# q, k and O turned by crossbar DMA transposes instead of TensorE, in an order made by a list scheduler

## The chip, the cores and the metric

The kernel runs on one core of one Trainium2 chip. The metric is device time in microseconds (us), the median of several executions. Here only fast runs are compared with fast runs; a run counts as slow when it is over 1.5% above the fastest of the same kernel. Engine names are those of the profile: PE is TensorE, PEld its weight loads, DVE is VectorE, ACT is ScalarE, POOL is GpSimd, SP is SyncE (here only an issuer of DMAs; SPq is its queue).

## The reference, cut to what matters

Sliding-window causal attention over 8 batches, 8 heads, 576 positions and 64 dimensions, with a window of 64 keys; the heads are then laid side by side as 4608 tokens of 512 features, which go through two dense layers with a SiLU between them. All inputs and the output are float32; both kernels compute in bf16.

```python
scores = scale * np.matmul(q, k.transpose(0, 1, 3, 2))
mask = (rel >= 0) & (rel < 64)                      # rel = query position - key position
attn = softmax(np.where(mask, scores, -1e9))
x = np.matmul(attn, v).transpose(0, 2, 1, 3).reshape(4608, 512)
h = x @ w_in                                        # 512 -> 2048, "first layer"
out = (h * sigmoid(h)) @ w_out                      # 2048 -> 512, "second layer"
```

## The kernel before

A *unit* is one pair of heads of one batch (32 units); a *group* is 192 query positions of a unit (96 groups); a *token tile* is 512 tokens (9 tiles, numbered from 0). The matmuls of both kernels are written for q and k with the 64 dimensions on the partitions, and those of the first layer for the attention output O with its features on the partitions, so all three are turned. Before, TensorE turns them: six matmuls against an identity for each q and k of a unit, three for the O of a group, each followed by an eviction from PSUM.

```python
def transposes(u, nm, copies):
    pst = at_ps.tile([128, 6, 96], BF16, name="pst", tag="ap")
    for m in range(6):
        nc.tensor.matmul(pst[:, m, :], lhsT=t[:, m, :], rhs=ident[0:96, 0:96], is_transpose=True, ...)
    # ... q: two evictions (VectorE, ScalarE) into qbd; k: one into kt

def scores(u, g):
    # ... three matmuls into sp
    nc.scalar.activation(out=e, in_=sp, func=ACTF.Exp, scale=scale)
    nc.vector.tensor_mul(e, e, mask0 if g == 0 else mask)

def values(u, g):
    # ... three matmuls into pv
    nc.vector.reciprocal(out=rc, in_=...)
    for hh in range(2):
        nc.vector.tensor_mul(ob[...], pv[...], rc[...].to_broadcast([64, 3, 64]))

def to_bridge(u, g):
    for x in range(3):
        nc.tensor.matmul(op[:, x, :], lhsT=ob[:, x, :], rhs=twoi, start=(x == 0), stop=(x == 2))
    nc.scalar.copy(out=bridge[pj][:, c0:c0 + 192], in_=op.rearrange("p x i -> p (x i)"))
```

The order is made by hand. The first layer of tile 0 is cut in two, so that it starts when the first 192 positions of batch 0 are there. After that, the q and k turns of the next units are placed among the first-layer matmuls of a tile, and 12 or 8 groups of attention among its second-layer matmuls:

```python
interleave(mm1(0, 0, 192), 7, first, lead=2)
# ...
for j in range(NTT):
    # ...
    interleave(mm1(j, 192, TT) if j == 0 else mm1(j), 6, ins, lead=30 if j == 0 else 4)
    interleave(mm2(j, j == 0), 3, attention_steps(part[j]), lead=2)
```

The softmax here doesn't subtract the row's maximum and nothing guards it: scores larger than these inputs give would overflow.

## Time and profile before

| | before |
|---|---|
| time, median of 3 | 396.05 us (395.33 to 396.76) |
| span of the profiled execution | 394.6 us |
| TensorE, VectorE, ScalarE, GpSimd busy | 329.4, 232.9, 206.3, 133.4 us |
| first matmul of the first layer | 41.5 us |
| first matmul of tile 1 | 89.2 us |

The last two rows are read from the timeline of TensorE. I use the second to cut every kernel into a **head** (start of the span to the first first-layer matmul of tile 1) and a **body** (from there to the end of the span): here 89.2 and 305.4 us.

These are lines of the page of the kernel before. The rows of digits are 40 equal slices, each digit the busy share of a slice in tenths; the rows with q0 and q1 are the DMA queues with packets, MB and share of the 16 DMA engines; the line after them is the chain that ended last, by engine; the last lines are groups of instructions (busy us and mean ns behind the bar, then the idle time before them). Of the names, e is the exponentials, pv the products with v, rc the reciprocals of their sums, obd (later ob) the normalised output, bridge the first layer's input, kraw a k that is turned but not yet in its place in kt.

```profile
PE 329.4 (83%) x2423; PEld 180.0 (46%) x2464; DVE 232.9 (59%) x596; ACT 206.3 (52%) x410; POOL 133.4 (34%) x185
...
PE   0046896999989997899779978998799889989995
...
DMA  9999999129901916382646456723710001001002
...
q0 software_dynamic: 45568, 11.28, 29.0%
q1 hardware_dynamic: 38336, 25.96, 24.4%
...
PE 51%; DVE 32%; ACT 6%; issue 5%; POOL 2%; DMA 2%; DVEq 0%; ACTq 0%; POOLq 0%
...
L169 DVE TENSOR_TENSOR e<-e,mask 128x384 bf16<-128x384 bf16 x96 | 43.0, 452 | 49.5 <-ACT e L168 47.1
L187 DVE TENSOR_TENSOR obd<-pv,rc 64x192 bf16<-64x192 f32 x192 | 68.2, 355 | 4.6
```

TensorE is close to full from the fifth slice on, and the DMA engines are full in the first seven slices (to about 69 us) and mostly half empty after that. The same in numbers, from the busy times by windows (after the window: us, busy us of the five engines with instruction counts, granted clock, DMA share, GB/s; the DMA share sums the time of packets and can be above 1):

```profile
0.00:41.50 41.50, 11.76 (x115) 9.32 (x116) 20.95 (x69) 15.39 (x28) 30.00 (x47) 0.99 1.24 205
...
89.20:268.00 178.80, 161.76 (x1185) 85.35 (x1208) 113.88 (x265) 101.81 (x193) 57.99 (x77) 1.00 0.55 109
```

In the head, the chain of the kernel before goes through a cast, six TensorE transposes and an eviction for each turn (start us, us, what):

```profile
8.91 7.15 DMA vv<-in_v_dram
...
19.75 0.42 DVE q_natb L126
20.22 0.68 PE pst L136 x6
20.92 0.75 DVE qbd L143
...
41.65 0.48 PE ps L226 x3
```

In a second-layer phase with 12 groups of attention, the chain that ended last runs through VectorE: reciprocal, two normalisations, mask, group after group. The columns are start us, us, and what.

```profile
149.54 0.21 DVE rc L184
149.77 0.04 DVE obd L187
149.81 0.33 issue
150.13 0.36 DVE obd L187
...
150.53 0.69 DVE ot L238
151.25 0.36 DVE e L169
```

Such a phase takes 25.9 us (141.9 to 167.8), of which TensorE is busy 21.0.

### The profile page before, as it was taken

The page shows a single profiled execution, that of the slowest core. Times are in us where ns is not written, and L with a number is a line of the kernel's source. Part 1 is how long each engine was busy: PE and PEld are TensorE (multiplying, and loading weights), DVE is VectorE, ACT ScalarE, POOL GpSimd, SP SyncE. Part 2 cuts the span into 40 slices and gives each one's busy share as a digit, 9 for nine tenths or more (in the row PEclk, how much of TensorE's full clock was granted, in tenths as well). Part 3 has the DMA queues.
Part 4 walks back from the last instruction along what each step waited for, and adds up shares of the span by engine and source line. Part 5 has one row for each costly group of instructions (what it writes and reads, how often), then busy time and mean ns, then how long its engine had stood idle before and what let it go on. Part 6 is the DMA issues. An engine that isn't in the chain of part 4 may idle for free.

```text
span 394.6 us, 6598 instructions
## 1 busy us (share of the span) xinstructions
PE 329.4 (83%) x2423; PEld 180.0 (46%) x2464; DVE 232.9 (59%) x596; ACT 206.3 (52%) x410; POOL 133.4 (34%) x185
## 2 busy tenths in 40 slices
PE   0046896999989997899779978998799889989995
PEld 0035773545454554354435543545355544454442
DVE  0467979967584649664984485539944790093011
ACT  2066775545842774367445752585357645742710
POOL 8756999123900029200950077004900000000000
PEclk9999899899999999999999999999999999999999
DMA  9999999129901916382646456723710001001002
GB/s 190 166 213 250 119 209 174 9 17 272 120 27 71 250 10 64 71 213 54 65 51 185 109 57 86 201 67 43 71 55 0 30 27 55 0 28 69 13 27 80
DMA packets 83935, 37.65 MB, mean 95 GB/s; under 512 B 40256, under 2 KB 78656, under 8 KB 83904
## 3 DMA queue, kind: packets, MB, share of 16 engines
q0 software_dynamic: 45568, 11.28, 29.0%
q1 hardware_dynamic: 38336, 25.96, 24.4%
q8 instruction: 19, 0.31, 0.3%
q14 instruction: 12, 0.10, 0.1%
HBM read 36.70 MB, written 9.44 MB: 117 GB/s over the span
## 4 chain that ended last, share of the span: by engine, by line
PE 51%; DVE 32%; ACT 6%; issue 5%; POOL 2%; DMA 2%; DVEq 0%; ACTq 0%; POOLq 0%
PE ps L226 28%; PE ps L250 15%; DVE obd L187 13%; DVE e L169 7%; DVE rc L184 4%; PE pst L136 4%; ACT L168 2%; DVE ot L238 2%; PE pv L177 2%; DMA vv<-in_v_dram 2%; ACT e L168 2%; DVE qbd L143 2%; ACT gt L233 1%; POOL vv L75 1%; DVE vv L151 1%
## 5 line engine op out<-in xcount | busy, mean ns | idle before, releaser
L250 PE MATMUL ps<-w_out_sb,gt 128*128 128x512 bf16 x551 | 141.5, 381 | 1.3 <-ACT gt L233 0.3
L226 PE MATMUL ps<-bridge,w_in_sb 128*128 128x512 bf16 (+2 forms) x624 | 135.2, 359 | 0.9
L233 ACT ACTIVATE gt<-ps 128x512 bf16<-128x512 f32 (+2 forms) x160 | 84.6, 555 | 46.8 <-PE ps L226 45.3
L75 POOL DMA_DIRECT2D vv<-in_v_dram x64 | 49.1, 773 | 131.4 <-PE pv L177 90.6
L226 PEld LDWEIGHTS <-w_in_sb 128*128 128x128 bf16 x640 | 58.8, 99 | 51.9 <-issue 0.8
L169 DVE TENSOR_TENSOR e<-e,mask 128x384 bf16<-128x384 bf16 x96 | 43.0, 452 | 49.5 <-ACT e L168 47.1
L187 DVE TENSOR_TENSOR obd<-pv,rc 64x192 bf16<-64x192 f32 x192 | 68.2, 355 | 4.6
L250 PEld LDWEIGHTS <-gt 128*128 128x128 bf16 x576 | 49.4, 98 | 41.1 <-issue 1.0
L168 ACT ACTIVATE e<-sp 128x384 bf16<-128x384 f32 x96 | 44.7, 491 | 33.9 <-PE sp L162 33.8
L238 DVE COPY ot<-ps 128x512 f32<-128x512 f32 x36 | 24.6, 690 | 55.9 <-PE ps L250 55.3
L202 ACT CAST bridge<-op 128x192 bf16<-128x192 f32 x96 | 30.6, 318 | 45.6 <-PE op L199 44.3
L177 PE MATMUL pv<-vv,e 128*128 128x130 bf16 x288 | 33.8, 228 | 11.9 <-DVE e L169 6.8
L144 ACT COPY qbd<-pst 64x576 bf16<-64x576 bf16 x32 | 20.3, 633 | 40.3 <-DVE qbd L143 40.3
L199 PE MATMUL op<-twoi,obd 128*128 128x64 bf16 x288 | 25.1, 197 | 17.9 <-DVE obd L187 15.5
L162 PEld LDWEIGHTS <-kt 128*128 128x128 bf16 x288 | 25.2, 104 | 24.0 <-issue 2.9
L136 PE MATMUL pst<-ident,q_natb 96*128 96x96 bf16 x192 | 14.4, 214 | 26.0 <-DVE q_natb L126 26.0
L162 PE MATMUL sp<-qbd,kt 128*128 128x128 bf16 x288 | 33.2, 231 | 3.1 <-ACT kt L147 1.4
L147 DVE COPY kt<-pst 128x576 bf16<-128x576 bf16 x28 | 21.1, 755 | 18.3 <-PE pst L136 18.3
L177 PEld LDWEIGHTS <-e 128*128 128x128 bf16 x288 | 21.9, 101 | 20.9 <-DVE e L169 10.8
L199 PEld LDWEIGHTS <-obd 128*128 128x128 bf16 x288 | 15.7, 99 | 33.2 <-DVE obd L187 32.8
L143 DVE COPY qbd<-pst 64x576 bf16<-64x576 bf16 x32 | 24.0, 749 | 11.1 <-PE pst L136 11.0
L126 POOL CAST q_natb<-q_nat 96x768 bf16<-96x768 f32 x28 | 24.7, 881 | 13.3 <-DMA q_nat<-in_q_dram 13.3
(37 smaller groups left out, 188.8 us busy)
## 6 DMA issues: line engine op xcount, KB each, us to landing
out_dram<-ot SPq DMA_DIRECT2D x36, 256.0 KB, 2.1
q_nat<-in_q_dram SPq DMA_DIRECT2D x28, 288.0 KB, 6.1
k_nat<-in_k_dram SPq DMA_DIRECT2D x28, 288.0 KB, 6.1
vv<-in_v_dram POOLq DMA_DIRECT2D x64, 64.0 KB, 3.3
w_in_sb<-in_moe_w_in_dram POOLq DMA_DIRECT2D x8, 256.0 KB, 7.5
w_out_sb<-in_moe_w_out_dram POOLq DMA_DIRECT2D x8, 256.0 KB, 7.1
q_nat<-in_q_dram POOLq DMA_DIRECT2D x4, 288.0 KB, 8.8
k_nat<-in_k_dram POOLq DMA_DIRECT2D x4, 288.0 KB, 9.0
```

The lines of the kernel that those rows point to most:

```text
L75: nc.gpsimd.dma_start(out=t[:, 1:9:2, hh * 65:hh * 65 + 64], in_=v[b, 2 * pj + hh, 0:512, :].rearrange("(c p) d -> p c d", p=128),)
L143: copies[0](out=d[0:64, 0], in_=src[0:64])
L162: nc.tensor.matmul(sp[:, x], lhsT=kt[i][:, t * 64:t * 64 + 128], rhs=qbd[i][:, :, t * 64:(t + 1) * 64], start=(x == 0), stop=(x == 2),)
L168: nc.scalar.activation(out=e, in_=sp, func=ACTF.Exp, scale=scale)
L169: nc.vector.tensor_mul(e, e, mask0 if g == 0 else mask)
L177: nc.tensor.matmul(pv[:, x, :], lhsT=e[:, x].rearrange("p h i -> p (h i)"), rhs=vv[i][:, 3 * g + x, :], start=(x == 0), stop=(x == 2),)
L187: nc.vector.tensor_mul(ob[p0:p0 + 64, :, p0:p0 + 64], pv[p0:p0 + 64, :, hh * 65:hh * 65 + 64], rc[p0:p0 + 64, :, hh:hh + 1].to_broadcast([ ...
L199: nc.tensor.matmul(op[:, x, :], lhsT=ob[:, x, :], rhs=twoi, start=(x == 0), stop=(x == 2))
L226: nc.tensor.matmul(ps[:, lo:hi], lhsT=w_in_sb[:, c, ft * 128:(ft + 1) * 128], rhs=bridge[c][:, t0 + lo:t0 + hi], start=(c == 0), stop=(c = ...
L233: nc.scalar.activation(out=gts[(j, ft)][:, lo:hi], in_=ps[:, lo:hi], func=ACTF.Silu)
L238: nc.vector.tensor_copy(out=ot, in_=ps)
L250: nc.tensor.matmul(ps[m], lhsT=gts[(j, f)][:, m * 128:(m + 1) * 128], rhs=w_out_sb[:, f, :], start=(f == 0), stop=(f == NFT - 1),)
```

## The change

The intent is to take 384 q and k transposes and 288 O turns off TensorE, and their evictions off VectorE and ScalarE, and to have the DMA do them from SBUF to SBUF with `dma_start_transpose` ("crossbar" transposes in what follows; 89 of them in the trace of the kernel after, whose result is correct): q straight into its place, k into a buffer from which VectorE copies it, O straight into the first layer's input. All of these transposes go through one queue, SP. The order of all work, on all engines and DMA queues, is no longer written by hand: a list scheduler runs before the kernel is built, with a duration for each operation, and issues in the order of its simulated clock.

The diff, cut to its core:

```diff
+class Plan:
+    def add(self, eng, cls, us, fn, deps=(), lat=0.08, gate=None, dma=None): ...
+    def run(self, rank):
+        # ... at each event, each free engine takes the ready operation with the lowest (rank, number)
+                    end = free[e] = now + op["us"]
+                    if op["dma"] is None:
+                        op["seen"] = end + op["lat"]
+                    else:
+                        pipe = max(pipe, end + 0.6) + op["dma"]      # one pipe for all DMAs
+                        op["seen"] = pipe + 1.2
...
-    def transposes(u, nm, copies): ...          # TensorE, PSUM, evictions
-    def to_bridge(u, g): ...                    # TensorE, PSUM, eviction
+    def turn_q(w, b, pj):                       # 48 rows, 24 blocks of 128 columns
+        nc.sync.dma_start_transpose(
+            out=qbd[b % NK][:, pj].rearrange("x h m p -> x (h m) p"),
+            in_=nbq[w][r:r + NPR].rearrange("p h m x -> p (h m x)"))
+    def turn_k(w, pj):                          # 48 rows, 12 blocks
+        nc.sync.dma_start_transpose(out=kraw[pj], in_=nbk[w][r:r + NPR].rearrange("p m x -> p (m x)"))
+    def place_k(eng, b, pj): ...                # VectorE copy kraw -> kt
+    def turn_o(o, b, g):                        # 64 rows, 12 blocks: 192 positions of all four head pairs
+                nc.sync.dma_start_transpose(
+                    out=bridge[:, a:z].rearrange("x n j i -> x (n j) i"),
+                    in_=obs[o % NOB][:, s:s + z - a].rearrange("p n j x -> p (n j x)"))
...
+                p.add("SP", "turn", 0.5, lambda pj=pj, w=w: turn_q(w, b, pj), cast_done[2 * pp] + busy, dma=1.0)
+                p.add("SP", "turn", 0.5, lambda pj=pj, w=w: turn_k(w, pj), ..., dma=0.5)
+            o_turn.append(p.add("SP", "turn", 0.5, lambda o=o, b=b, g=g: turn_o(o, b, g), ..., dma=0.8))
...
-    interleave(mm1(0, 0, 192), 7, first, lead=2)   # and the loop over tiles
+    p.run(dict(one=0, ld=3, turn=0, st=2, dma=1, cast=5, shift=4, place=3, s=1, pv=0, moe=3, exp=1, silu=0,
+               mask=1, norm=0, out=2))
```

Three smaller things come with it. The loads of q and k bring packets of 1 KB instead of 512 B, and v comes in one layout for all heads of a batch. The casts to bf16 run on ScalarE (on GpSimd before, after the first units). The first layer of tile 0 is no longer cut in two: it waits for all of batch 0.

## The prediction

> **What bounds the kernel now.** The page gives TensorE 83% busy, VectorE 59%, ScalarE 52%, DMA 53% by queue shares. The 1,152 MoE matmuls set the floor: where they run back to back (last tile, timeline 376.8 on: 16 in 3.45 us) one takes 0.216 us, 249 us in all. The other 146 us are three things.
>
> 1. Head: the first MoE matmul starts at about 41 us (timeline). VectorE waited 12.5 us for v loads merely to write ones columns (waits: vv L121), so its first q cast came at 19.7. The first token tile is then cut in two and mixed with attention; tile 1 starts only at 89.
> 2. Each later token tile takes 34 to 42 us (chain: 126.2, 168.0, 209.8, 247.7, 288.9) against 27.7 for the last one, which has nothing beside it. Six TensorE transposes cost 0.26 us of the stream (first-layer phase: groups of six matmuls every 1.55 instead of 1.30), 2 per head pair, up to 2.1 us a tile. The O turn costs about 0.1 us a group, scores plus values 0.36.
> 3. TensorE waits in second-layer phases for VectorE: 1.36 us a group (mask 0.452, reciprocal 0.194, two normals 0.355 each). One 12-group phase takes 26 us for 18 us of MoE and attention matmuls. The chain holds obd 13%, mask 7%, rc 4%.
>
> **Removed.** PE: 384 transposes (28.8 us busy) and 288 O turns (25.1 us). VectorE: q evictions 24.0 us, most clears; ScalarE: q evictions 20.3, bridge copies 30.6. PSUM buffers for both turns vanish.
>
> **Added.** 32 q, 32 k and about 25 O crossbar transposes on the SP queue, 18.9 MB. This trace has none. [...] each plus about 2 us to land (stores land in 2.1). No run here shows it yet. q/k packets double from 512 B to 1 KB[...]. ScalarE takes the casts (0.83 us each by the k cast seen here, about 50 us): its total stays near 205. VectorE falls from 233 to about 205.[...]
>
> **Critical path.** Clears precede v loads, so casts start near 6 us; turns, then 12 groups x 1.36 us on VectorE, then an O turn: first MoE matmul near 38 us, now with batch 0 complete. After it 249 us of MoE, 84 groups x 0.34 = 29 us of attention matmuls, 4 us tail: 320. Mismatch of the static order with real DMA latency, one exposed O turn before tile 1, and DMA contention: about 15 us more. **335 us, 8 in 10 between 313 and 372**; faster 0.87, same 0.06, slower 0.07. A 15% gain.
>
> **What would show it.** First MoE matmul at 34 to 44 us; tile 1 starting at 70 to 78, not 89; tiles of 30 to 34 us; TensorE gaps over 0.4 us largely gone beside attention; VectorE busy 195 to 215; O turns landing 2.5 to 4 us after issue; DMA share up to 60 to 80%.
>
> **What would make it wrong.** Transposes moving under about 100 GB/s: then q/k turns of a batch take over 20 us, the head grows by 10 to 20 us, and SP, in order, holds stores and loads behind them; the chain would show DMA qbd, kraw or bridge. Priorities tuned on wrong durations would show as PE waiting for ScalarE's casts ahead of silu (0.83 us each), or for bridge. If turns are faster and the model exact, 313.

The sum came to 320 us: 38 for the head, 249, 29 and 4; with about 15 more it is 335.

## The result and the profile after

| | before | after |
|---|---|---|
| time, median of 4 | 396.12 us (395.33 to 396.76) | 437.94 us (433.73 to 441.35) |
| span of the profiled execution | 394.6 us | 434.7 us |
| TensorE, VectorE, ScalarE, GpSimd busy | 329.4, 232.9, 206.3, 133.4 us | 308.0, 192.4, 192.0, 45.8 us |
| first matmul of the first layer | 41.5 us | 87.0 us |
| head (to tile 1) | 89.2 us | 127.5 us |
| body | 305.4 us | 307.2 us |

The change is slower: the ratio is 1.102, 95% interval 1.093 to 1.111. A ratio is the mean time of one kernel's fast runs over the mean of the other's fast runs of the same rounds, so it is not quite the ratio of the medians that I quote. (One of the four executions of after, the 441.35, counts as slow and is not in the ratio.) The result is correct in both.

So of the 40.1 us between the two spans, 38.3 are in the head and 1.8 in the body. Two things have to be explained: why the head grew, and why the body gained nothing although TensorE has less to do there.

The page of the kernel after, the lines that answer to those above:

```profile
PE 308.0 (71%) x1706; PEld 151.8 (35%) x1728; DVE 192.4 (44%) x484; ACT 192.0 (44%) x316; POOL 45.8 (11%) x55
...
PE   0000033099949999992999299969988868799996
...
DMA  9999999999896999799679997969742482401001
...
q1 hardware_dynamic: 100000, 46.02, 62.2%
q0 software_dynamic: 43776, 8.92, 26.7%
q10 hardware_dynamic: 1664, 1.57, 2.4%
...
L216 DVE COPY kt<-kraw 128x576 bf16<-128x576 bf16 x32 | 35.7, 1128 | 62.2 <-DMA kraw<-nbk 62.0
```

TensorE is idle or nearly so for eight slices, and later its row has single low digits (4, 2, 2), where before it has none below 7 from the eighth slice to the last but one. The DMA row is full or nearly so over two thirds of the span. The queue shares add up to 91%, where before they were 53%.

```profile
0.00:87.00 87.00, 9.78 (x73) 6.87 (x74) 26.55 (x72) 17.30 (x26) 25.89 (x35) 1.00 1.42 179
...
127.50:300.00 172.50, 147.72 (x828) 72.19 (x839) 92.51 (x232) 97.08 (x161) 15.96 (x16) 0.92 1.04 151
```

The clock of 1.00 in the first line says nothing: the first clock record of this trace is at 91 us.

The chain that ended last, in the head of the kernel after:

```profile
4.67 10.26 DMA nat<-in_q_dram
...
15.43 0.56 DVE nbq L201
16.01 1.79 SPq L205
17.84 6.46 SPq L205
...
34.24 6.15 SPq L205
40.44 8.48 SPq L205
...
49.65 1.40 SPq L212
51.10 9.28 DMA kraw<-nbk
60.41 1.13 DVE kt L216
61.58 0.82 PE sp L232 x6
...
77.10 9.74 DMA bridge<-ob
86.98 3.15 PE mp L277 x7
```

This is how to read it. The first q load lands at 15.0, its cast is done at 16.0. Then SP, which issues in program order, is held: L205 is the issue of one q transpose, and the four of batch 0 hold the queue for 1.8, 6.5, 6.2 and 8.5 us. They come in two pairs, each with its two k transposes (L212) behind it and with loads of batch 1 (L164) between. The last k transpose lands at 60.4, 9.3 us after its issue. Two groups of batch 0 have run by then (from 40.6); the ten that are left take 16.7 us, 1.67 us a group, and the last O transpose 9.7 us more. In the kernel before, the first q turn ran from 20.2 to 21.7 with its eviction, 1.5 us.

The waits of the kernel after (engine, line, what it waited for: us in all, times, longest) name the same two places:

```profile
PE sp L232 <- DVE kt L216: 66.9, 9, 40.6
DVE kt L216 <- DMA kraw<-nbk: 62.0, 15, 14.4
...
PE mp L277 <- DMA bridge<-ob: 26.8, 6, 11.6
```

In the body, five first layers wait for an O transpose (1.0 to 5.7 us each), and what follows a wait can start slowly. From the timeline of TensorE (start us, us, ..., count, then idle before and what ended it):

```profile
205.13 2.29 PE L277 MATMUL mp<-bridge,w_in_sb 128*128 128x512 bf16 x5 [5.65 <-DMA bridge<-ob]
```

Five matmuls took 2.29 us. At the full rate they take 1.08 (16 in 3.45 us on the last tile before). In this trace the granted clock is 0.50 from 200.25 to 210.49 us, so it came back 5.4 us after the matmuls began; it had fallen 0.8 us into the idle stretch, before which TensorE already had gaps of 0.95 and 2.15 us. The mean granted clock is 0.92 from 127.5 to 300 us, where the kernel before has 1.00. So this wait for DMA cost more than its own length: about 2.7 us more, an estimate (half of the 5.4 us at half clock). Over the body the clock stood at half for 38.6 us, in which TensorE was busy for 26.7; by the same estimate about 13 us are lost there.

### The profile page after: what moved, and what is told of

It reads as the page before. It is cut to its first block, busy times and chain, and to the rows that moved or that the text cites. A ratio compares the mean times of both kernels' runs of the same rounds, so it can differ in the third digit from the quotient of the medians.

```text
span 434.7 us, 4930 instructions
## 1 busy us (share of the span) xinstructions
PE 308.0 (71%) x1706; PEld 151.8 (35%) x1728; DVE 192.4 (44%) x484; ACT 192.0 (44%) x316; POOL 45.8 (11%) x55
## 3 DMA queue, kind: packets, MB, share of 16 engines
q0 software_dynamic: 43776, 8.92, 26.7%
## 4 chain that ended last, share of the span: by engine, by line
PE 56%; DMA 19%; DVE 11%; SPq 9%; issue 3%; ACT 2%; ACTq 0%; DVEq 0%
PE mp L277 30%; PE mp L286 19%; DMA bridge<-ob 9%; SPq L205 5%; DMA kraw<-nbk 5%; DVE ob L259 4%; DMA nat<-in_q_dram 3%; PE sp L232 3%; PE pv L249 3%; DVE kt L216 3%; SPq L212 2%; DVE ot L292 2%; DMA qbd<-nbq 1%; DVE rc L256 1%; SPq L164 1%
## 5 line engine op out<-in xcount | busy, mean ns | idle before, releaser
L277 PE MATMUL mp<-bridge,w_in_sb 128*128 128x512 bf16 x576 | 140.2, 404 | 34.8 <-DMA bridge<-ob 26.8
L283 ACT ACTIVATE g<-mp 128x512 bf16<-128x512 f32 x144 | 85.2, 597 | 134.6 <-PE mp L277 134.6
L286 PE MATMUL mp<-w_out_sb,g 128*128 128x512 bf16 x554 | 138.9, 381 | 1.2 <-issue 0.2
L286 PEld LDWEIGHTS <-g 128*128 128x128 bf16 x576 | 54.2, 98 | 50.8 <-issue 0.6
L259 DVE TENSOR_TENSOR ob<-pv,rc 64x192 bf16<-64x192 f32 x192 | 68.0, 354 | 4.6
L216 DVE COPY kt<-kraw 128x576 bf16<-128x576 bf16 x32 | 35.7, 1128 | 62.2 <-DMA kraw<-nbk 62.0
L292 DVE COPY ot<-mp 128x512 f32<-128x512 f32 x36 | 24.2, 689 | 85.1 <-PE mp L286 84.6
L201 ACT CAST nbq<-nat 112x768 bf16<-112x768 f32 x28 | 22.6, 827 | 18.6 <-DMA nat<-in_q_dram 14.6
L256 DVE RECIPROCAL rc<-pv 128x6 f32<-128x6 f32 x96 | 18.8, 195 | 26.5 <-PE pv L249 24.5
L199 ACT CAST nbk<-nat 112x768 bf16<-112x768 f32 x32 | 25.4, 830 | 11.2 <-DMA nat<-in_k_dram 10.4
L283 ACT ACT_TABLE_LOAD x8 | 10.3, 1283 | 0.1
```

The costliest lines, as they stand in the source:

```text
L199: eng(out=dst[:, h], in_=src[:, h])
L216: eng(out=kt[b % NK][:, 64 + pj * S:64 + (pj + 1) * S].rearrange("x (g p c) -> x g p c", g=NG, c=NC), in_=kraw[pj].rearrange("x (g c) p -> ...
L259: nc.vector.tensor_mul(obs[o % NOB][:, :, pj, 64 * hh:64 * hh + 64], pv[r, :, hh, 0:D], rc[r, :, hh:hh + 1].to_broadcast([64, 3, 64]),)
L277: nc.tensor.matmul(mps[mp], lhsT=w_in_sb[:, c, ft * 128:(ft + 1) * 128], rhs=bridge[:, n0:n0 + TB, c, :], start=(c == 0), stop=(c == NDC - 1),
L283: nc.scalar.activation(out=gts[gt], in_=mps[mp], func=ACTF.Silu)
L286: nc.tensor.matmul(mps[mp], lhsT=gts[gt][:, m * 128:(m + 1) * 128], rhs=w_out_sb[:, f, :], start=(f == 0), stop=(f == NFT - 1),)
```

## The experiments

Four theories, with what each would show:

- **The crossbar is slow in these shapes.** Alone on an idle DMA the transposes are already far slower than I had taken them to be. Then other shapes, or plain copies of the same bytes, give the time back.
- **The DMA is full.** The turns are late because loads lie ahead of them and beside them. Then taking loads away, or moving them, gives the time back.
- **The order is built on wrong durations.** The scheduler believes in 1.0 us for a q turn. Then true durations give a better order.
- **The O turn is the body's wait.** Then a first layer that does not wait for it gives the body's loss back.

The expectations are quoted; where they name a theory by a letter, C is the one of the wrong durations and F one that came up later, that the casts on ScalarE delay the rest. What each run was to tell apart is said in words beside it.

All results in one table. Ratios are against the kernel before in the same rounds; head and body are from the profiled execution of each, as defined above. Of the six of late, two were slow and are not in its ratio.

| run | what it is | us, median | ratio (95%) | head | body |
|---|---|---|---|---|---|
| before | | 396.12 | 1 | 89.2 | 305.4 |
| after | | 437.94 | 1.102 (1.093–1.111) | 127.5 | 307.2 |
| copy* | after, turns replaced by plain copies | 412.40 | 1.039 (1.033–1.044) | 125.8 | 283.5 |
| wide | after, turns of 128 rows | 409.54 | 1.033 (1.029–1.037) | 128.3 | 279.4 |
| no_w* | after, weights not loaded | 418.69 | 1.056 (1.051–1.062) | 111.1 | 305.9 |
| no_v* | after, v of batches 2 to 7 not loaded | 426.86 | 1.079 (1.073–1.084) | 123.2 | 298.9 |
| no_o_wait* | after, first layer reads a constant | 421.61 | 1.063 (1.059–1.068) | 123.5 | 296.0 |
| replan | after, true durations in the scheduler | 471.32 | 1.187 (1.179–1.195) | 142.8 | 327.1 |
| late | after, loads of batches 1, 2 later | 435.29 | 1.090 (1.083–1.097) | 127.0 | 308.8 |
| wide_late | wide and late | 402.58 | 1.017 (1.011–1.023) | 121.6 | 279.0 |
| wl_pool | wide_late, casts on GpSimd | 408.56 | 1.027 (1.022–1.033) | 124.6 | 282.4 |
| mix | wl_pool, q/k of batch 0 and all O on TensorE | 414.79 | 1.046 (1.042–1.049) | 117.4 | 295.4 |
| pe_all | after, all turns on TensorE | 415.87 | 1.048 (1.043–1.053) | 95.0 | 319.1 |
| pe_rank | pe_all, evictions ranked first | 406.61 | 1.025 (1.021–1.028) | 96.2 | 308.8 |
| pe_pool | pe_rank, casts on GpSimd | 434.15 | 1.095 (1.091–1.098) | 112.3 | 319.8 |
| pe_tab | pe_pool, table loads in the scheduler | 426.55 | 1.075 (1.070–1.079) | 115.6 | 310.0 |
| clear_first | before, clears ahead of v loads | 395.39 | 0.997 (0.993–1.002) | 90.0 | 305.4 |
| bias | before, mask added by a matmul | 366.13 | 0.923 (0.919–0.927) | 84.1 | 280.7 |
| wide_bias | wide_late, mask added by a matmul | 406.61 | 1.026 (1.022–1.030) | 122.4 | 281.9 |

A star marks kernels whose result is wrong. All others computed the right result.

### The cost of a transpose alone

A kernel that only moves data: each shape first alone, then eight of it in a row, on a DMA with nothing else to do. Its output is wrong, which doesn't matter for the time.

```python
train(turn_dense, 8, 48, 24)     # q: 48 rows, 24 blocks
train(turn_dense, 8, 48, 12)     # k
train(turn_dense, 8, 64, 12)     # O
train(turn, 8, 128, 12)          # 128 rows
train(copy, 8, 9)                # plain copy of q's bytes in packets of 256 B
```

> Wrong result on purpose: nothing but DMAs, each shape twice alone and then eight in a row, on an otherwise idle chip. Theory A (the crossbar transpose is slow by itself): a row of eight q shapes (48 rows x 24 blocks of 128) moves under 150 GB/s, about 110 as in the trace of the changed kernel at 340 to 357 us (a q turn every 2.6 us), while plain copies of the same bytes in the same 256 B packets run at 200 GB/s or more. Theory B (it is fast alone and only suffers from other traffic): q shapes at 250 GB/s or more, one every 1.2 us.

For scale: the two busiest slices in the page of the kernel before moved 250 and 272 GB/s.

One issue of each row, once the queue is full, from the chain of this run (start us, us, what); in order a q shape, a k shape, an O shape, 128 rows, and a plain copy:

```profile
60.57 2.71 SPq L37
...
79.17 1.29 SPq L37
...
93.02 1.44 SPq L37
...
106.26 1.80 SPq L33
...
125.17 1.32 SPq L40
```

The spacing of the landings over each row of eight is 2.69 us for q (295 KB, 110 GB/s), 1.42 for k (147 KB, 104 GB/s), 1.49 for O (197 KB, 132 GB/s), 1.84 for 128 rows (393 KB, 213 GB/s) and 1.38 for the plain copy (295 KB, 214 GB/s). So a crossbar transpose was as fast as the copy with 128 rows (213 against 214 GB/s), and about half as fast with 48 (110). The transposes of the change add up to 32 × 2.69 + 32 × 1.42 + 25 × 1.49 = 168.8 us of an otherwise idle DMA.

What makes the narrow rows slow is not shown. In a row of q the DMA engines were busy for 0.74 of the time only (0.70 for k, 0.83 for O), with 128 rows for 1.14; the windows of q and of 128 rows (after the window: us, busy us of VectorE and GpSimd, clock, DMA share, GB/s):

```profile
55.20:68.70 13.50, 0.77 (x5) 0.00 (x0) 1.00 0.74 109
...
106.20:115.50 9.30, 0.77 (x5) 0.00 (x0) 1.00 1.14 212
```

And one transpose alone, on an empty queue, already held SP for 1.2 us (k, O) to 1.3 us (q), where a plain copy held it for 0.6 to 0.7. For k and O the issue alone is most of the spacing (1.2 of 1.42 and 1.49 us). So a slow crossbar and a slow issue are both possible, and the runs below do not separate them: plain copies are issued faster, and turns of 128 rows need fewer issues (57 instead of 89). "Slow shape" stands for either. In the kernel after, among its other traffic, one q turn held SP for up to 8.5 us, and a k turn landed 4.5 us after its issue in the median and 13.5 at the longest.

### Plain copies in place of the transposes, and the transposes with 128 rows

copy moves the same bytes through the same queue in the same order, without the crossbar:

```diff
-        nc.sync.dma_start_transpose(
-            out=qbd[b % NK][:, pj].rearrange("x h m p -> x (h m) p"),
-            in_=nbq[w][r:r + NPR].rearrange("p h m x -> p (h m x)"),
+        nc.sync.dma_start(
+            out=qbd[b % NK][:, pj].rearrange("x h m p -> x (h m p)").rearrange("x (a y) -> x a y", y=128),
+            in_=nbq[w].rearrange("p h m x -> p (h m) x")[:, 0:18:2],
         )
 # ... and the same for k and O
```

> Wrong result on purpose: every crossbar transpose is a plain SBUF to SBUF copy of the same bytes in packets of about 256 B, issued from the same queue at the same place, with the same waits. Theory A (the crossbar itself is slow): the time falls by 40 us or more, to under 400, first MoE matmul before 65 us. Theory B (the volume on DMA queues that are already full, whatever kind): within 15 us of the changed kernel, 425 to 440. Theory C (the order made from wrong durations): like B, within 15 us.

wide keeps the crossbar and gives it 128 rows: two head pairs of q or k in one transpose without the zero blocks (VectorE then places q as well as k), and the head pairs of an O stacked two by two on 128 partitions:

```diff
+    def turn(raw, nb):
+        nc.sync.dma_start_transpose(out=raw, in_=nb.rearrange("p m x -> p (m x)"))     # 128 rows, 12 blocks
+    def place_q(b, pp, h):
+        nc.vector.tensor_copy(out=qbd[b % NK][x, 2 * pp:2 * pp + 2, h], in_=qraw[pp][x]...)
...
-                    in_=obs[o % NOB][:, s:s + z - a].rearrange("p n j x -> p (n j x)"),    # 64 rows
+                    in_=obs[o % NOB][:, s:s + z - a].rearrange("p n a x -> p (n a x)"),    # 128 rows
```

> Correct result. Same order rules and the same durations given to the scheduler, but each crossbar turn has 128 rows: two head pairs of q (without the zero halves) or of k at once, and O as 128 rows x 6 blocks instead of 64 x 12. VectorE places q as well as k (about 16 us more of it). Theory A' (the shape is what is slow: 48 rows at 110 GB/s, 128 rows at 213 in the probe): 395 to 415, like the plain copies (412). Theory C (order): 425 or more.

copy measured 412.4 and wide 409.5: the slow shapes are worth 25 to 28 us. Nearly all of it lies in the body (307.2 to 283.5 and 279.4). For wide that was expected; copy was to gain 40 us or more with a first first-layer matmul before 65 us, and missed both (25.5 us, 85.1). The head does not move (125.8 and 128.3, from 127.5). So the shape matters in the body and not in the head. wide, which also moves fewer bytes of q, is as good as copy: the crossbar as such is not what costs, its use in narrow shapes is. And the body of wide is 26 us shorter than that of the kernel before: with turns of 128 rows, taking them off TensorE does pay in the body.

### The weights, and v, not loaded

```diff
     def load_w_in(f):
-        nc.gpsimd.dma_start(...)
+        nc.gpsimd.memset(w_in_sb[:, :, f * 256:(f + 1) * 256], 0.03)      # and the same for w_out
```

> Wrong result on purpose: the changed kernel, with both weight tensors filled by memset instead of loaded (16 loads, 8.4 MB read, fewer in the first 60 us). Theory B (in the head the turns queue behind loads on full DMA queues): the first MoE matmul moves from 87 us to 70 or earlier and the time falls by 15 us or more. Theory A (the 48-row crossbar shape is slow whatever else runs): the head loses less than 8 us, 430 or more.

The first first-layer matmul came at 70.0 instead of 87.0 and the head was 111.1 instead of 127.5; the body did not move. The second pair of q transposes held SP for 8.0 us instead of 14.7. So the loads of the weights (8.4 MB of float32) are 16 us of the head. The other 22 us (111.1 less 89.2) are there without them.

no_v takes the loads of v for batches 2 to 7 away, to see whether it is the traffic in the body that makes the turns late there:

```diff
     def load_v(b, part):
+        if b >= NK:
+            return
```

> Wrong result on purpose: the changed kernel without the loads of v for batches 2 to 7 (24 of 32 loads, 27,648 of 145,464 DMA packets, all after the head); old values of v are used, every other operation and the order stay. Theory B, in its last form (after the head the DMA queues pace the changed kernel, at 90% or more of their time up to 300 us): the head stays (first MoE matmul 87 us, tile 1 at 127), the body from tile 1 to the end shrinks by 15 us or more from 303, the time to 422 or less. Rival (VectorE, the order): within 8 us of 438.

It gave 11 us, 8 of them in the body, which is between what the theories expected. The waits for the turns remained (VectorE waited 78.6 us for k transposes, in the kernel after 62.0). So this traffic is a part of the body's loss and not most of it.

### The first layer does not wait for O

The first layer reads a tile that is never written again; the order of all instructions stays:

```diff
-            rhs=bridge[:, n0:n0 + TB, c, :], start=(c == 0), stop=(c == NDC - 1),
+            rhs=still[:, :, c, :], start=(c == 0), stop=(c == NDC - 1),
```

> Wrong result on purpose: the first layer reads a constant tile instead of the turned O; every operation stays, in the same static order, only its wait for the O turn is gone. Theory D (each token tile is a serial chain: first layer, attention paced by VectorE in the second-layer phase, then the landing of the O turn): the waits for the turned O (26.8 us, 9.7 of them in the head) go and the time falls by 20 to 35 us, to 402 to 418. Rival (those waits only hide others that end just after: q and k turns, PSUM): less than 8 us.

It measured 421.6, 16.3 us less, 11.2 of them in the body; 20 to 35 us had been expected if each tile were such a chain. The waits for O in the body are 26.8 − 11.6 = 15.2 us in the trace of the kernel after (the longest is the head's), and the slow clock comes on top (about 2.7 us after the wait shown above, by the estimate there). So these waits are a real part of the loss, but taking them all away does not bring the body down to what the shapes alone are worth. That the turns of q and k delay it too is my reading; no run takes away their waits alone.

### True durations in the scheduler

```diff
-                p.add("SP", "turn", 0.5, lambda pj=pj, w=w: turn_q(w, b, pj), ..., dma=1.0)
+                p.add("SP", "turn", 2.0, lambda pj=pj, w=w: turn_q(w, b, pj), ..., dma=2.75)
-                p.add("SP", "turn", 0.5, lambda pj=pj, w=w: turn_k(w, pj), ..., dma=0.5)
+                p.add("SP", "turn", 1.3, lambda pj=pj, w=w: turn_k(w, pj), ..., dma=1.4)
 # ... O 1.25 and 1.75; q/k loads 1.25; v 2.9; weights 2.1; place_k 1.13
```

> Only the durations that the list scheduler is given are changed, to those that the trace shows (q turn 2.0 us on the queue and 2.75 of the DMA engines instead of 0.5 and 1.0; k 1.3 and 1.4; O 1.25 and 1.75; loads 1.25, k placement 1.13). Theory C (the order is the fault): 25 us or more come back, to 410 or less. Theories A and B (the turns cost what they cost): less than 12 us come back, 425 or more.

It is the worst kernel, 471.3. This theory fell in the form in which I had put it: better single durations did not give a better order. Why the order became so bad I have not settled. One thing visible in the trace is that the chain now has 9% in waits for v loads and 4% in waits for w_in, which in the chain of the kernel after do not show.

### Loads moved, in the head of the kernel after

```diff
+    def after_first(b):      # loads of batch 1 behind the turns of batch 0, those of batch 2 behind its O turns
+        ...
+        return held if b == 1 else o_turn[:3] if b == 2 else []
...
-                             cast_done.get(i, []), dma=0.83) for pj in (2 * pp, 2 * pp + 1)]
+                             cast_done.get(i, []) + after_first(b), dma=0.83) for pj in (2 * pp, 2 * pp + 1)]
```

> Correct result. The changed kernel with one rule more for its scheduler: the q and k loads of batch 1 come behind all q and k turns of batch 0 in the order, those of batch 2 behind the O turns of batch 0 (the queue that issues them is in order, so the order holds on the chip). Theory E (the head is long because loads that nobody needs yet sit in front of the turns of batch 0 in one in-order queue): first MoE matmul from 87 us to 60 to 72, tile 1 from 127 to 105 to 115, time down by 12 to 25 us. Rival (the head is bound by the total DMA volume, so deferred loads only come back as a wait before tile 1): first MoE matmul earlier, but tile 1 within 5 us of 127 and the time within 6 us.

> Correct result. The 128-row turns and the later loads together. If the two causes are separate (shape in the body, order of loads in the head), the gains add: 409.5 less the 12 to 25 us of theory E, 385 to 397, which is at or below the kernel before the change (396). If they are one cause, it stays above 402.

In the trace of late SP kept the order: the last k turns of batch 0 from 40.2 us, the loads put behind them from 45.9. late brought the first first-layer matmul from 87.0 to 77.8, and tile 1 still began at 127.0: what the head gained at its start it gave back before its end, since the loads that were put back were those of batch 1, and tile 1 needs batch 1 (in the trace of late the chain before tile 1 now has a q load of 5.0 us and an O turn of 8.7). In total nothing (435.3 against 437.9, ratios with overlapping intervals). On top of wide the same edit gained 7 us (402.6), all in the head (128.3 to 121.6); 12 to 25 had been expected of both.

clear_first tries the same place in the kernel before. Its clears wait for loads of v on buffers which they share; here they run first.

```diff
     consts()
+    for i in range(4):
+        zeros(i)
     for u in range(4):
         load_v(u)
     load_w_in()
-    for i in range(4):
-        zeros(i)
```

> The kernel before the change with one part of the change alone: the clears of the v buffers are issued ahead of the loads of v, so VectorE no longer waits for the loads (12.5 us) before the first q cast. My theory: the first MoE matmul moves from 41 us to 30 to 36, and the time falls by 5 to 12 us, to 385 to 391. Rival (the head is bound by the DMA, which is at 90% or more): less than 3 us.

The first first-layer matmul moved from 41.5 to 31.2, tile 1 from 89.2 to 90.0, and the time not at all (0.997; 5 to 12 us had been expected). It is the same finding in another kernel: an earlier first matmul is not a shorter head.

### Casts on GpSimd, and a mixture of both ways to turn

wl_pool moves the casts after batch 0 from ScalarE to GpSimd; mix also turns q and k of batch 0, and every O, on TensorE.

```diff
                 eng, fn, us = ("ACT", nc.scalar.copy, 0.85)
+                if b:
+                    eng, fn, us = ("POOL", nc.gpsimd.tensor_copy, 1.0)
```

> Correct result. wide_late (402.6 us) with the casts of batches 1 to 7 moved from ScalarE back to GpSimd, where the kernel before had them. Theory F (casts that wait for a late load stand in front of silu and exp in ScalarE's in-order queue; 86 to 92 us of wide_late shows one): first-layer phases shorten from 16 to 19 us to 14 to 16 and the time falls by 6 to 15 us, to 388 to 397. Rival (ScalarE is not on the chain in most tiles, VectorE and the O turn are): less than 4 us.

> Correct result. As wl_pool, but the turns whose landing is on the chain are done on TensorE: q and k of batch 0, and every O; the prefetched q and k of batches 1 to 7 stay on the crossbar with 128 rows. Theories A' and D together (crossbar good where the latency is hidden, bad where work waits for it): first MoE matmul at 50 to 58 us instead of 76, tile 1 near 97, waits for the turned O under 10 us in sum, and 362 to 380 us, faster than both kernels. If the loss is in the static order alone: 395 or more.

wl_pool was slower (408.6 against 402.6), so the casts on ScalarE were not what held the body; on GpSimd they stand in one queue with the loads of v. mix was to keep the best of both and to come near 370; it measured 414.8. Its first first-layer matmul was early (54.7), but its head stayed at 117.4, and in its trace TensorE waits up to 13.2 us for a mask: VectorE, in program order, stood before it at a shift of v whose load had taken 22.5 us to land.

### All turns back on TensorE, in the scheduler's order

This separates the two halves of the change. pe_all has the scheduler, the new layouts and the new loads, but TensorE does the turns, into one PSUM bank that the scores give up (they keep one of two), from which VectorE and ScalarE evict.

```diff
+    def pe_turn_qk(tp, w, kk, g):
+        for c in range(NC):
+            nc.tensor.matmul(t[:, c, 0:64 + NPR], lhsT=src[0:64 + NPR, NC * g + c, :],
+                             rhs=ident[0:64 + NPR, 0:64 + NPR], is_transpose=True, ...)
 # ... evictions; the same for O; ranks tq=2, to=0, evo=0
```

> The list scheduler and its order rules stay; q, k and O are turned on TensorE through one PSUM bank (scores get one bank instead of two). Theories A and B (the turns on the DMA are the loss): 340 to 365 us, first MoE matmul before 45, below the kernel before the change. Theory C (the static order is the fault): 400 or more, since the same scheduler and durations made it.

pe_all measured 415.9: a head of 95.0, and a body of 319.1. By its time this is what had been expected if the static order is the fault (400 or more), not if the turns on the DMA are the whole loss (340 to 365); only its head speaks for the turns. I had ranked the evictions behind other work, so that the one bank stayed taken; pe_rank puts them first, pe_pool then moves the casts to GpSimd, and pe_tab tells the scheduler of the ScalarE table loads (1.28 us each, 15 in the trace of the kernel after), of which its model knows nothing.

```diff
-    p.run(dict(..., place=3, ..., tq=2, to=0, evo=0))
+    p.run(dict(..., place=-1, ..., tq=2, to=0, evo=-1, evq=-1))        # pe_rank
```

```diff
+                    if c in ("exp", "silu") and table != c:            # pe_tab, on top of pe_pool
+                        table = c
+                        end = free[e] = end + 1.28
```

> Correct result. pe_all (416 us) with one fault of my own version repaired: the evictions that hold its single PSUM bank get the first rank on VectorE and ScalarE instead of the last. If pe_all lost because O turns bunched behind that bank (2.6 to 4 us without matmuls before each first-layer phase, and then half the granted clock for 2 us): 8 us or more faster, to 408 or less. Rival (the order itself): within 4 us.

> Correct result. pe_rank, and the casts of batches 1 to 7 on GpSimd, where the kernel before had them. Theory F (casts in ScalarE's queue stand in front of silu: first-layer phases of 19 us in pe_all against 16 before): phases of 16 to 17 us and 6 to 15 us less than pe_rank. Rival (VectorE paces the tile): less than 3 us. If it comes below 396 the scheduler's order is no worse than the order by hand, and the whole loss of the change is the turns and the place of the casts; if it stays above 402, the order loses by itself.

> Correct result. pe_pool, and the scheduler's model is told of the 1.28 us that ScalarE takes to change between exp and silu, which it leaves out. Theory G (a static order fails where its model leaves out a wait: PE stands at the start of each second-layer phase behind the first exp): 4 us or more less than pe_pool. Rival: within 3 us.

pe_rank gained 9 us (406.6), so that was my fault and not the scheduler's. pe_pool lost 28, pe_tab won 8 of them back. With turns on TensorE the scheduled order has a head of 96.2 and a body of 308.8, against 89.2 and 305.4 by hand. So the scheduled kernel gains nothing without the DMA turns; it stands about 10 us behind the order by hand. How much of that is the order is not shown, since the single banks, the casts on ScalarE, the layouts and the uncut first layer differ too. Changes of rank, of a modelled duration or of the engine of the casts move it between 406.6 and 434.2, and its head between 95.0 and 115.6 with no transpose on the DMA at all. Why, I leave open.

### VectorE in the kernel before

The last question was whether something in these traces beats both kernels. In the body of the kernel before, the second-layer phases are paced by VectorE (1.36 us a group: mask 0.452, reciprocal 0.194, two normalisations of 0.355). bias moves one VectorE operation per group to TensorE: the mask is no longer multiplied after the exponential, but added before it, as 0 or −2048, by a matmul against the identity into the same PSUM tile. Scaled by 1/8 it is −256 in the exponential, which has to give 0 (the result of bias is correct).

```diff
-        nc.gpsimd.memset(m2, 1.0)
+        nc.gpsimd.memset(m2, 0.0)                       # and fill=-2048.0 outside the window
...
         sp = at_ps.tile([128, 3, 2, 64], FP32, name="sp", tag="ap")
+        nc.tensor.matmul(sp, lhsT=ident, rhs=mask0 if g == 0 else mask, start=True, stop=False)
         for x in range(3):
...
-                start=(x == 0), stop=(x == 2),
+                start=False, stop=(x == 2),
...
         nc.scalar.activation(out=e, in_=sp, func=ACTF.Exp, scale=scale)
-        nc.vector.tensor_mul(e, e, mask0 if g == 0 else mask)
```

> Correct result. The kernel before the change, with the mask moved from VectorE to TensorE: one matmul of an identity with a tile of 0 and -2048 starts the PSUM bank, the scores accumulate on it, exp gives the zeros; VectorE loses 96 multiplications (43 us), TensorE gains 96 matmuls of 384 columns (0.16 us each, 15 us). Theory H (in both kernels VectorE paces the second-layer phases at 1.36 us a group): phases of 12 groups shorten from 26 us to 20 to 22, and the time falls to 362 to 380, below both kernels. Rival (TensorE or the DMA paces them): 392 or more.

It measured 366.13 (364.96 to 367.53), ratio 0.923, faster than both kernels. Its page, and its timeline at the start of a second-layer phase:

```profile
PE 331.2 (91%) x2560; PEld 187.6 (51%) x2560; DVE 189.7 (52%) x500; ACT 202.5 (56%) x410; POOL 131.4 (36%) x185
...
PE 82%; DMA 10%; POOL 4%; DVE 1%; issue 1%; ACT 1%; POOLq 0%; ACTq 0%
```

```profile
135.15 0.33 PE L160 MATMUL sp<-mask,ident 128*128 128x384 bf16 x1
135.31 0.33 PE L163 MATMUL sp<-qbd,kt 128*128 128x128 bf16 x3
135.48 0.81 PE L250 MATMUL ps<-w_out_sb,gt 128*128 128x512 bf16 x3
```

The added matmul costs TensorE 0.16 us of its stream (135.15 to 135.31), 96 times, and takes 0.452 us off VectorE. The chain, which before had 32% on VectorE, now has 1% there and 82% on TensorE. The second-layer phase that took 25.9 us takes 20.9 (134.5 to 155.4). The body is 24.7 us shorter, the head 5.1.

wide_bias does the same in wide_late:

> Correct result. wide_late (402.6 us) with the same move of the mask. If VectorE's pace in the second-layer phase is a link of the chain there too, 378 to 395. If the body of that kernel is paced by the DMA, which is at 90% or more up to 270 us, within 6 us of 402.6.

There it gains nothing (406.6 against 402.6). The same move is worth 30 us in the kernel before, where VectorE paces the phase, and nothing there; that the turns pace it instead fits the alternative, but this run does not show which of them. The operation is also cheaper there: a mask takes 0.355 us in wide_late, 0.452 in the kernel before. Casts on GpSimd may be part of that difference: pe_pool, which differs from pe_rank in nothing else but them and the order that follows, has 0.426 against 0.355; wl_pool has only 0.359 against the 0.355 of wide_late.

## Why the prediction was wrong

The prediction said 335 us, between 313 and 372; it was 437.9. Point by point:

- **What bounds the kernel before: right.** Point 3 of the prediction put the excess of the second-layer phases on VectorE, at 1.36 us a group. bias takes 0.452 us of it away and the kernel gets 30 us faster.
- **The cost of the transposes: wrong, and the first step that failed.** I took one rate for all shapes, which no run had shown. The shapes here run at 104 to 132 GB/s when alone: 2.69, 1.42 and 1.49 us, 168.8 in all. wide and copy show what that term is worth in the whole kernel: 25 to 28 us, nearly all of it in the body.
- **"First MoE matmul near 38 us": wrong by 49 us, and the larger error.** It was 87.0. I added the lengths of the operations, each with about 2 us to land. The chain has three DMA trips where I counted little: 10.3 us for the load, the SP queue held until the k turn could be issued at 51.1 and landed at 60.4, and 9.7 us for the O turn. The page of the kernel before shows seven full DMA slices at just this place; the turns moved there did not take their own length (a pair of q turns held SP for 14.7 us, without the weight loads for 8.0). no_w shows 16 us of it as the weight loads, in an unchanged order. pe_all shows the whole: with the turns on TensorE and the rest of the change kept, the head is 95.0 instead of 127.5. By this difference turning by DMA costs 32 us there, and the rest of the change about 6 (95.0 less 89.2); it is a difference between two orders, and pe_pool, with turns on TensorE too, has a head of 112.3.
- **"Tiles of 30 to 34 us": wrong.** From tile 1 to tile 7 a tile took 40.8 us on average (127.5 to 372.5 in six), before 39.9 (89.2 to 328.6 in six). What was removed from TensorE was less than its busy time: by my own estimates in the prediction, 64 turns at 0.26 us and 96 at 0.1 are 26 us of the stream, not 54, and 48 and 72 of them, about 20 us, lie in the body. Against it stand the waits for O turns (15.2 us in the body), the waits for q and k turns, and the half clock (about 13 us, as estimated above). In the body TensorE was busy for about 11 us less than before and idle about 13 us more (busy times by windows, 89.2 to 391 and 127.5 to 431). The gain was there: with turns of 128 rows the body is 26 us shorter than before. In the change as it was made, the slow shapes ate it.
- **"O turns landing 2.5 to 4 us after issue": wrong.** The median is 5.3 us, from 3.1 to 11.6.
- **DMA share "up to 60 to 80%": too low.** The queues add up to 91%. **VectorE busy 195 to 215, ScalarE near 205: about right**, 192.4 and 192.0. A k placement takes 1.13 us, where the scheduler had been given 0.7.
- **"What would make it wrong" named the case that happened**, transposes near 100 GB/s with SP holding everything behind them, and put 10 to 20 us on the head for it. It was 38. I gave a slower kernel a chance of 0.07 only, since I took my rate for the transposes as if it had been measured on these shapes. The probe would have told in one run.
- **The scheduler.** I expected its order to be off by up to about 15 us. With the turns on TensorE its kernel is about 10 us slower than the one by hand, not all of it shown to be the order. But my picture that true durations would mend it was wrong (replan, 471.3).

So the 42 us are 38 of head and a body in which gain and loss cancel. In the head, about 32 us come from turns that queue on a full DMA and in one in-order queue (16 of them shown by no_w, the rest by the difference to pe_all), and about 6 from the rest of the change. In the body, about 20 us less matmul work on TensorE (an estimate) and 30 us less on VectorE (172.5 to 142.7 us busy) came to nothing, and the slow shape of the transposes is worth 24 to 28 us there (by copy and wide). The attribution by differences of whole kernels is rough, since each variant also gets another order from the scheduler where its durations or dependences change; copy, no_w, no_v and no_o_wait keep the durations and the order.

What stays open: whether the narrow transposes are slow in the crossbar or in their issue; why true durations gave a worse order; why the scheduled kernel with the turns on TensorE stays 10 us above the one by hand; and how the 22 us of head that are left without weight loads divide between the queue and the other traffic. Two kernels that were to answer the last (late, mix) gave back later what they had gained early.

## What to carry to other kernels

A unit of work that is moved to the DMA has to be costed by its shape, alone, in a probe (here 104 to 213 GB/s by shape), and then by what the DMA is already doing at the very moment when the critical chain needs it; the page's row of DMA slices says that, and an average share does not (before: seven full slices at this place, 53% by the queue shares). A chain of short on-chip steps that became a chain of DMA trips got the latency of each trip (10.3, 9.3 and 9.7 us), and the SP queue, in order, passed the delay of one on to all behind it (14.7 us for one pair of q turns). When a step of the start-up gets earlier, look for the next fixed point (here tile 1) before counting the gain; and when an engine paces a phase, moving one of its operations to the engine that waits for it can be worth more than taking work off the busiest one (30 us in bias).
